# Attention by runs of the sequence and list-scheduled engine orders in a fused attention and hyena kernel

## The chip, the cores and the metric

The kernel runs on one core of one Trainium2 chip. The metric is the device time of one execution in microseconds (us). The kernel before took 243.26 us (median of three executions, 241.11 to 243.58) when the prediction was made.

The engines are called as the profile calls them. PE is the tensor engine with its matmuls, and PEld its weight loads. DVE is the vector engine, ACT the scalar engine, POOL the engine that issues the casting loads, and SP the engine that issues the other loads and the stores. PSUM is the memory that PE writes. It has eight banks, each of 512 float32 values per partition. ACT and DVE read it and so make room for PE.

## The reference

Attention with a window of 96 positions and 8 global positions feeds a projection into three parts. The second part is convolved with a filter along the sequence, which the kernel does as a product of spectra, with the Fourier transforms as matmuls. The other two parts are its gates.

```python
# q, k, v: 4 batches, 8 heads, 768 positions, 64 columns
scores = q @ k.T / 8 - slope[head] * dist        # only kept positions: local or global
a = exp(scores - max); a = a / sum(a)
x = (a @ v), heads side by side                  # 4 x 768 x 512
x1, x2, x3 = split(x @ w_proj)                   # 512 columns each
x2_conv = irfft(rfft(x2) * rfft(filter_fft))     # along the 768 positions
out = (x1 * x2_conv * x3) @ w_out
```

## The kernel before

Everything is issued in an order woven by hand. One batch is attention, head pair by head pair, and then a "hyena" stage: the projection of x2, its spectrum, the product with the filter, the inverse, the gates, and the last projection. The attention of batch b + 1 is woven into the hyena stage of batch b. The gates `x1 * x3` are handed out wherever the stage would let PE wait.

```python
def mm(self):                                   # single-bank products: three banks of their own
    pt = self.ps.tile([P, 512], F32, tag="mm", bufs=3)
    return pt
# scores:     self.ps.tile([P, 2, 512], F32, tag="s",  bufs=1)   one tile of two banks, read as a whole
# values:     self.ps.tile([P, 7, D + 1], F32, tag="av", bufs=2)
# transposes: self.ps.tile([P, 1024], F16, tag="tr", bufs=1)

def gate(j, s):                                 # half s of the sequence, 128 columns j
    p1 = self.mm()
    p3 = self.mm()
    for pt, o in ((p1, 0), (p3, 2 * DM)):
        for c in range(4):
            nc.tensor.matmul(pt[:, 0:h], self.w[:, c, o + P * j:o + P * j + P],
                             xT[:, c, h * s:h * s + h], start=(c == 0), stop=(c == 3))
    x1 = mp.tile([P, h], F16, tag="x1", name="x1")
    nc.scalar.mul(x1, p1[:, 0:h], X1_SCALE)
    nc.vector.tensor_mul(g[:, j, h * s:h * s + h], p3[:, 0:h], x1)

# in the hyena stage ... (cut)
for s in range(6):
    self.forward(s, ab[0], ab[1], evac)         # spectrum of x2
    yield 1
    if s % 2 == 1 and s > 1 and more():         # more(): the next gate, if one is left
        yield 1
for _ in range(2):
    if more():
        yield 1
# ... inverse, with more() between its halves, then the last projection (cut)
```

Attention 0 also issues matmuls on an idle tile (`self.busy(1)`), 38 in all, to keep PE busy. The Fourier tables are computed after attention 0.

The softmax here doesn't subtract the row's maximum and nothing guards it: scores larger than these inputs give would overflow.

## Time and profile before

One execution is read here, with a span of 240.6 us.

| what | value |
|---|---|
| busy | PE 83%, DVE 67%, ACT 60%, POOL 31% |
| attention 0 alone | 0 to 45 us |
| tables, filter, hyena stage 0, attention 1 | 45 to 119 us |
| two mixed periods | 43.7 us each, PE busy 41.5 us in each |
| last hyena stage, alone | 34 us |

The page of the kernel before, its totals and some of its rows of 40 slices (each digit is the busy share of 6 us in tenths; PEclk is the granted clock of PE in tenths):

```profile
span 240.6 us, 4274 instructions
PE 200.6 (83%) x1664; PEld 108.8 (45%) x1664; DVE 161.1 (67%) x334; ACT 144.4 (60%) x232; POOL 75.2 (31%) x102
...
PE   4575968887978665867999999899999997999883
...
PEclk9998597997999995697999999999999999999999
DMA  6999999999991000002999910033000002400006
```

The same execution by stretches. The columns are the stretch, its length, the busy time of PE, PEld, DVE, ACT and POOL with instruction counts, the granted clock, the DMA share and GB/s:

```profile
0.00:45.00 45.00, 31.16 (x278) 16.84 (x278) 30.27 (x70) 21.58 (x28) 35.63 (x55) 0.89 2.00 191
45.00:119.00 74.00, 57.44 (x452) 30.70 (x452) 49.98 (x95) 44.09 (x71) 27.90 (x35) 0.88 1.11 66
119.00:162.70 43.70, 41.62 (x395) 23.43 (x394) 33.09 (x71) 29.98 (x51) 11.66 (x14) 1.00 1.26 99
162.70:206.40 43.70, 41.45 (x391) 23.09 (x388) 33.08 (x71) 29.84 (x50) 0.00 (x0) 1.00 0.10 35
206.40:240.60 34.20, 28.88 (x154) 14.71 (x152) 14.69 (x27) 18.94 (x35) 0.00 (x0) 1.00 0.18 67
```

The two periods in the middle are bound by PE, which is busy for 95% of them. The first 119 us are not. There PE waits, as the chain of waits (start, length, work) of the stretch from 53 us shows, where tables, filter and products follow each other through three engines:

```profile
53.07 1.28 ACT L267
54.36 2.40 ACT fwd L267 x4
57.77 0.70 DVE h_767 L358
58.49 0.59 ACT h_767 L360
```

### The profile page before, as it was taken

Reading aid. Unit: us, or ns where it says so; the run is one execution under the profiler, and the core shown is the slowest. Engines: PE = TensorE matmul, PEld = TensorE weight load, DVE = VectorE, ACT = ScalarE, POOL = GpSimd, SP = SyncE. Lnnn points to the kernel's source line nnn. Section 1 sums busy time; section 2 is a strip of 40 time slices with the busy share of each in tenths; the row PEclk is TensorE's granted clock in tenths of the full one; section 3 lists DMA queues with packets and bytes.
Section 4 is the critical chain, followed back from the end, with each engine's and each line's share of the span. In section 5 each row is a group of like instructions: output and inputs, shape, how many; then the busy total and the mean of one; then the engine's idle time right before and its main releaser. Section 6 shows DMA issues by size and latency. Waiting matters only on the chain.

```text
span 240.6 us, 4274 instructions
## 1 busy us (share of the span) xinstructions
PE 200.6 (83%) x1664; PEld 108.8 (45%) x1664; DVE 161.1 (67%) x334; ACT 144.4 (60%) x232; POOL 75.2 (31%) x102
## 2 busy tenths in 40 slices
PE   4575968887978665867999999899999997999883
PEld 1333545332445342544545565455556554455541
DVE  5587586683675896597246999943599994139550
ACT  4462574477553863573668748466866765774643
POOL 6969478987930000004977200000000000000000
PEclk9998597997999995697999999999999999999999
DMA  6999999999991000002999910033000002400006
GB/s 190 347 132 197 204 155 149 122 171 148 129 119 11 0 3 0 3 0 18 191 246 142 114 10 3 0 143 123 0 3 0 4 0 102 162 0 0 3 34 229
DMA packets 79572, 21.68 MB, mean 90 GB/s; under 512 B 71328, under 2 KB 76480, under 8 KB 79552
## 3 DMA queue, kind: packets, MB, share of 16 engines
q0 software_dynamic: 73584, 11.67, 86.1%
q1 hardware_dynamic: 5968, 9.74, 12.2%
q8 instruction: 13, 0.21, 0.4%
q14 instruction: 7, 0.06, 0.1%
HBM read 26.48 MB, written 6.29 MB: 136 GB/s over the span
## 4 chain that ended last, share of the span: by engine, by line
PE 47%; DVE 23%; ACT 10%; issue 3%; ACTq 0%; DVEq 0%
PE pt L552 9%; PE pt L566 9%; PE pt L649 8%; PE pt L631 5%; PE pt L323 4%; DVE g L557 3%; DVE xn L527 3%; PE sp L490 3%; ACT E_99 L497 3%; PE tx L534 2%; PE o L517 2%; PE o L522 1%; PE tk L478 1%; PE tq L453 1%; DVE X L592 1%
## 5 line engine op out<-in xcount | busy, mean ns | idle before, releaser
L552 PE MATMUL pt<-xT,w 128*128 128x384 f16 x256 | 47.8, 331 | 2.1 <-ACT x_861 L556 1.7
L552 PEld LDWEIGHTS <-w 128*128 128x128 f16 x256 | 24.1, 99 | 18.8 <-issue 4.4
L497 ACT ACTIVATE E_99<-sp 128x864 f16<-128x864 f32 x24 | 21.5, 897 | 13.4 <-PE sp L490 12.7
L649 PE MATMUL pt<-wo,y 128*128 128x512 f16 x96 | 24.4, 396 | 2.6 <-DVE y L642 2.6
L497 ACT ACTIVATE E_96<-sp 128x864 f16<-128x864 f32 x24 | 21.5, 894 | 7.7 <-PE sp L490 7.6
L105 POOL DMA_DIRECT2D vt<-in_v_dram x28 | 25.1, 911 | 2.6 <-DMA kt<-in_k_dram 1.2
L490 PE MATMUL sp<-QT,KT 64*128 64x216 f16 (+2 forms) x224 | 18.5, 258 | 6.4 <-ACT E_99 L497 2.6
L631 PE MATMUL pt<-inv,X 128*128 128x384 f16 x96 | 20.6, 351 | 3.7 <-DVE X L592 3.6
L652 ACT ACTIVATE t<-pt 128x512 f32<-128x512 f32 x24 | 14.3, 597 | 13.7 <-PE pt L649 13.6
L105 POOL DMA_DIRECT2D kt<-in_k_dram x21 | 18.9, 916 | 6.8 <-DMA qt<-in_q_dram 3.3
L527 DVE TENSOR_TENSOR xn<-o,rc 128x448 f16<-128x448 f32 x32 | 20.0, 625 | 1.1
L568 ACT CAST dst<-pt 128x512 f16<-128x512 f32 x24 | 14.1, 587 | 8.8 <-PE pt L566 8.8
L323 PE MATMUL pt<-dst,fwd 128*128 128x512 f16 x72 | 18.9, 380 | 0.0
L275 PE MATMUL pt<-idle 128*128 128x512 f16 x38 | 17.7, 503 | 1.2 <-DVE idle L674 1.2
L535 ACT COPY xT<-tx 128x768 f16<-128x768 f16 x16 | 12.8, 798 | 8.5 <-PE tx L534 8.4
L490 PEld LDWEIGHTS <-KT 64*128 64x128 f16 x224 | 7.8, 96 | 21.9 <-issue 18.6
L595 ACT CAST X<-pt 128x512 f16<-128x512 f32 x24 | 14.1, 587 | 4.9 <-PE pt L323 4.6
L534 PE MATMUL tx<-ident,xn 128*128 128x128 f16 x112 | 9.8, 232 | 8.1 <-DVE xn L527 8.1
L118 POOL DMA_DIRECT2D qt<-in_q_dram x18 | 15.9, 904 | 0.2 <-issue 0.2
L96 POOL MEMSET vt<- 128x56 f16 x4 | 1.6, 412 | 43.3 <-PE o L522 43.3
L649 PEld LDWEIGHTS <-y 128*128 128x128 f16 x96 | 9.1, 102 | 13.2 <-DVE y L642 4.0
L631 PEld LDWEIGHTS <-X 128*128 128x128 f16 x96 | 8.9, 103 | 11.1 <-DVE X L592 4.7
(231 smaller groups left out, 393.5 us busy)
## 6 DMA issues: line engine op xcount, KB each, us to landing
out_dram<-t SPq DMA_DIRECT2D x24, 256.0 KB, 2.6
vt<-in_v_dram POOLq DMA_DIRECT2D x24, 128.0 KB, 7.0
qt<-in_q_dram POOLq DMA_DIRECT2D x18, 128.0 KB, 8.2
kt<-in_k_dram POOLq DMA_DIRECT2D x18, 128.0 KB, 6.5
t<-in_q_dram SPq DMA_DIRECT2D x4, 384.0 KB, 6.1
t<-in_k_dram SPq DMA_DIRECT2D x4, 384.0 KB, 7.1
w<-in_moe_w_proj_dram POOLq DMA_DIRECT2D x3, 512.0 KB, 9.7
fl<-in_moe_filter_fft_dram POOLq DMA_DIRECT2D x1, 768.0 KB, 10.4
```

What stands on the lines that cost most here:

```text
L105: g.dma_start(dst[P - (hi - lo):P, t, :, 0:D], src[b, :, lo:hi, :].rearrange("h p d -> p h d"))
L118: g.dma_start(qt[:, t], self.q[b, :, P * t:P * t + P, :].rearrange("h p d -> p h d"))
L275: self.nc.tensor.matmul(pt, self.idle[:, 0:P], self.idle, start=True, stop=True)
L323: self.nc.tensor.matmul(pt, self.fwd[:, kt, s, :], src[:, kt, :], start=(kt == 0), stop=(kt == 2))
L490: nc.tensor.matmul(sp[:, hh, off:off + w], KT[64 * hh:64 * hh + 64, o:o + P], QT[64 * hh:64 * hh + 64, KL * m:KL * m + w], start=(off == 0 ...
L497: nc.scalar.activation(eo, sp[:, :, 0:432].rearrange("p h (m w) -> p h m w", m=2), Act.Exp, scale=self.scale)
L527: nc.vector.tensor_mul(xn[:, :, hh, :], o[:, :, 0:D], rc.to_broadcast([P, 7, D]))
L534: nc.tensor.transpose(tx[:, KL * t:KL * t + P], xn[:, t, :, :], self.ident)
L552: nc.tensor.matmul(pt[:, 0:h], self.w[:, c, o + P * j:o + P * j + P], xT[:, c, h * s:h * s + h], start=(c == 0), stop=(c == 3))
L566: nc.tensor.matmul(pt, src[:, c, P * t:P * t + P], self.w[:, c, DM:2 * DM], start=(c == 0), stop=(c == 3))
L631: nc.tensor.matmul(pt[:, 0:h], X[:, s, cs], self.inv[:, s, :], start=(s == slots[0]), stop=(s == slots[-1]))
L649: nc.tensor.matmul(pt, y[:, c, P * t:P * t + P], self.wo[:, c, :], start=(c == 0), stop=(c == 3))
```

## The change

Its intent is to let nothing wait for an order fixed by hand. Each operation is handed to a list scheduler with a cost, what it reads and what it writes. The scheduler chooses the order of every engine, which of ACT and DVE empties a bank, and the bank. Attention goes by three runs of the sequence over all head pairs. A run's gates are made as soon as its x is transposed, and no longer inside the hyena stage (now `conv`). Angles and sines of the tables come first, under the first loads. The idle matmuls are gone. The diff of some 1,500 lines, cut to its core:

```diff
+class Plan:                                     # list scheduler (cut)
+    def schedule(self):
+        banks = [0.0] * 8                       # when each of 8 banks is free
+        ...
+                if o.acq:
+                    if o.acq.n == 1:            # a single bank: any of the eight
+                        i = min(range(8), key=lambda i: (max(banks[i], at), banks[i ^ 1] == math.inf
+                                                          and -1 or 0, -banks[i]))
+                    else:                       # scores take two
+                        i = min((0, 2, 4, 6), key=lambda i: max(banks[i], banks[i + 1]))
+        ...
+        self.psum = [self.ps.tile([P, 1024], F32, name=f"bank{i}") for i in range(4)]
+    def emit(self, order):
+        for o in order:
+            a = o.acq
+            if a:
+                lo = 512 * (a.at % 2)
+                a.tile = self.psum[a.at // 2][:, lo:lo + 512 * a.n]
+            o.fn(o.eng)
+
+    def attention(self, b):
+        for c in range(3):                      # runs of the sequence
+            ...                                 # transposes of Q and K, scores, values, transposes of x
+            if c:
+                for j in range(4):
+                    self.gate(b, j, c - 1)      # gates as soon as the run is there
-    def mm(self):
-        pt = self.ps.tile([P, 512], F32, tag="mm", bufs=3)
-        return pt
-        gates = iter([(j, s) for j in range(4) for s in range(2)])
-        def more(): ...                         # gates handed out inside the hyena stage
-                    if first:
-                        self.busy(1)            # idle matmuls
```

## The prediction

> **What bounds the kernel now.** The table of stretches splits the 240.6 us span. 0 to 45 us: attention of batch 0 alone (PE busy 31.2 us, much of it fillers on an idle tile; granted clock 0.89). 45 to 119 us: filter tables, gating stage 0 and attention 1 (PE busy 57.4 of 74 us, clock 0.88). 119 to 206.4 us: two periods of 43.7 us (PE busy 41.5 each, clock 1.00: bound by the tensor engine). Then the last gating stage alone (PE busy 28.9 of 34.2). DVE (67%) and ACT (60%) bound no long stretch. In the first 66 us the page's DMA slices read 9 at some 180 GB/s, about 150 where casting loads run alone: the start is bound by loads, then by the serial chain of filter tables and products (chain of waits, 53 to 95 us), with PE waiting for DVE and ACT.
>
> **What the matmuls need.** From spacings in the timeline (0.216 us at 512 columns, 0.162 at 384, about 0.032 for value products, 0.058 for transposes, score pairs side by side): gating stage 28.7 us, attention 10.3, filter 5.8; 163 us in all. A period's floor is 39 against 43.7.
>
> **What the change does.** Matmuls stay (1,630 in the order listing against 1,664, 38 fillers gone). Sines and forward tables move ahead of attention 0, under the first loads. Gates follow each run of x; conv 0, filter and attention 1 interleave freely; any free PSUM bank serves any product. Some 37 of 52 Q and K copies go to ACT: ACT grows from 144 to about 157 us busy, DVE stays near 161 (16 more reciprocals at 0.2 us, more small copies). Batch 0's Q and K lose their contiguous load: Q comes in 256 byte pieces, K is cast by the POOL queue.
>
> **Sum.** Loads until batch 1's values: Q 1.6 MB at about 300 GB/s, 7 MB by POOL at 150: about 55 us. By then the order has 44 us of PE work. 119 us remain: 101 in mixed periods, which I stretch by 9% (before: 12%) to 110, and the last conv, now without gates to fill its waits: 9.1 (projection, forward) + 4.6 (evacuation, products, sums) + 3.9 + 1.6 + 5.2 + 3.6 (evacuation, store) = 28 us. 55 + 110 + 28 + 2 for a throttled clock = **195 us**, range **186 to 209**. Nearly all the gain lies in the first 119 us (now 75 to 80 for the same work); mixed periods give 2 to 4 us each.
>
> The Trainium skill (TensorE: Matmul & The Clock Gate, Part 1) says that about 3.4 us idle halves the clock. The dips in the clock slices fit; without fillers I expect dips before 35 us.
>
> Chances: faster 0.94, same 0.03, slower 0.03.
>
> **What would show it.** PE busy about 180 us, over 90% from 55 us to the last conv, clock 1.00 there; DMA slices at 9 until about 55; periods of 41 to 43 us; PE waits of 4 to 5 us on DVE sums in the last conv; no long PE wait on ACT sines.
>
> **What would make it wrong.** The fixed orders: if loads land late, PE stands behind a transpose of batch 1 while gates could run (PE waiting for DMA). Small Q pieces slower than 300 GB/s. DVE and ACT, some 80% busy in a shorter span, holding banks (PE waiting for evacuations), so that periods stay at 44. Throttling in 20 to 55 us. Each costs 5 to 15 us.

## The result, and the profile after

The kernel after is correct and takes 234.2 us (median of four executions, 232.63 to 234.45). The kernel before, timed on the same chip in the same rounds, took 242.7 us. The ratio is 0.9651, with a 95% interval of 0.9598 to 0.9705. Ratios in this document are the mean time of one kernel's fast runs over that of the other's fast runs of the same rounds, so they are not quite the ratio of the medians quoted. The change is faster by 3.5%. The predicted 195 us, with a range of 186 to 209, is far off. Most of the expected gain is missing.

The page of the kernel after, same rows as before:

```profile
span 232.7 us, 4288 instructions
PE 190.6 (82%) x1630; PEld 111.4 (48%) x1630; DVE 157.6 (68%) x381; ACT 145.1 (62%) x252; POOL 75.0 (32%) x96
...
PE   5473889798996797899989998999979889991871
...
PEclk9997667999999599999999999999999999999799
DMA  7999999999999979992400000150000001500015
```

The stretches of the kernel after. The last three begin with the conv of batch 1, 2 and 3, up to a microsecond or two:

```profile
0.00:55.00 55.00, 40.60 (x370) 26.68 (x371) 40.86 (x109) 33.86 (x53) 45.11 (x63) 0.88 2.02 167
55.00:113.30 58.30, 49.70 (x444) 29.60 (x442) 41.11 (x96) 38.03 (x70) 29.87 (x34) 0.94 1.44 109
113.30:156.20 42.90, 39.85 (x362) 22.89 (x362) 31.74 (x77) 30.29 (x54) 0.00 (x0) 1.00 0.10 38
156.20:200.30 44.10, 40.39 (x371) 23.62 (x371) 33.38 (x79) 29.43 (x52) 0.00 (x0) 1.00 0.09 32
200.30:232.60 32.30, 20.05 (x87) 8.63 (x85) 10.52 (x20) 13.54 (x27) 0.00 (x0) 0.94 0.19 71
```

PE lost its idle matmuls, but its busy share did not rise. The mixed periods take 43 and 44 us, as before, with PE busy for 92 to 93% of them (95% before). The last conv has PE busy for only 20 of 32 us, where the last stage before had 29 of 34. Its gates, some 10 us of matmuls, are already done, and still it is only 2 us shorter.

Where the trace says that engines waited (engine, tile and line, then what for; us in total, times, longest us), five lines of the kernel after:

```profile
ACT x L310 <- PE bank L682: 14.4, 17, 2.7
...
ACT eo L306 <- PE bank L746: 10.5, 11, 5.7
...
DVE p L795 <- ACT X L306: 10.9, 2, 8.8
...
PE bank L746 <- DVE X L806: 3.7, 1, 3.7
...
PE bank L552 <- DMA kn<-in_k_dram: 3.0, 2, 1.9
```

PE names no single long wait: the largest is 3.7 us, once, in the last conv. So the loss is spread over many short waits, and one has to ask for a reason that acts everywhere. The first line gives a hint. ACT copies the first product of a gate, x1, and waits for PE on it 17 times. Looking at single ones, such a copy often starts 0.65 us later than its own product ends, which is the time of four matmuls of 384 columns: the length of the next product.

One more figure serves below. "PE's own work" is the sum over matmuls started of their spacing at full clock (0.216 us for 512 columns, 0.162 for 384, 0.056 for 128, 0.030 for a value product, score pairs counted side by side). It is 161.1 us for the whole kernel after. The prediction said that 44 us of it would be in the order by 55 us. The trace has 26.8 us of it by then. The other 134.3 us then take 177.7 us, so 1.32 us per us of work, where the prediction had (110 + 28 + 2) / 119 = 1.18. With that rate 26.8 us by 55 us would have given about 213 us. So of the miss of 37.7 us in the span, about 18 lie in the first 55 us and about 20 in the rate after them.

### The profile page after: what moved, and what is told of

It is laid out like the page before. It is cut to its first block, busy times and chain, and to the rows that moved or that the text cites. A ratio compares the mean times of both kernels' runs of the same rounds, so it can differ in the third digit from the quotient of the medians.

```text
span 232.7 us, 4288 instructions
## 1 busy us (share of the span) xinstructions
PE 190.6 (82%) x1630; PEld 111.4 (48%) x1630; DVE 157.6 (68%) x381; ACT 145.1 (62%) x252; POOL 75.0 (32%) x96
## 5 line engine op out<-in xcount | busy, mean ns | idle before, releaser
L682 PE MATMUL bank<-xT,w 128*128 128x384 f16 x256 | 44.3, 329 | 2.6 <-ACT xT L306 1.4
L588 ACT ACTIVATE E<-bank 128x864 f16<-128x864 f32 x48 | 40.1, 903 | 1.6 <-PE bank L578 1.4
L682 PEld LDWEIGHTS <-w 128*128 128x128 f16 x256 | 25.1, 99 | 19.9 <-issue 3.6
L600 DVE TENSOR_TENSOR E<-E,mask 128x864 f16<-128x864 f16 x32 | 18.4, 602 | 17.8 <-ACT E L588 17.7
L322 POOL DMA_DIRECT2D kn<-in_k_dram x28 | 25.4, 920 | 5.5 <-DMA g<-in_moe_filter_fft_dram 2.9
L322 POOL DMA_DIRECT2D vn<-in_v_dram x28 | 25.0, 914 | 2.3 <-PE bank L625 1.4
L746 PE MATMUL bank<-inv,X 128*128 128x384 f16 x96 | 20.9, 364 | 5.4 <-DVE X L806 3.7
L769 PE MATMUL bank<-wo,y 128*128 128x512 f16 x96 | 22.5, 379 | 2.4 <-ACT eo L306 1.0
L640 DVE TENSOR_TENSOR xn<-bank,rc 128x256 f16<-128x256 f32 (+1 forms) x48 | 22.5, 469 | 1.6
L310 ACT ACTIVATE ot<-bank 128x512 f32<-128x512 f32 x24 | 13.4, 595 | 14.3 <-PE bank L769 6.8
L620 PE MATMUL bank<-vn,E 128*128 128x65 f16 x224 | 18.8, 201 | 2.3 <-DVE xn L640 0.7
L539 PE MATMUL bank<-ab,fwd 128*128 128x512 f16 x72 | 18.3, 379 | 1.3 <-ACT ab L306 0.7
L625 PE MATMUL bank<-vn,E 128*128 128x65 f16 x192 | 18.5, 200 | 0.0
```

The costliest lines, as they stand in the source:

```text
L310: self.nc.scalar.mul(out, in_, c)
L322: return self.g.op(eng, {"G": 0.93, "S": 0.5}[eng], lambda _: e.dma_start(dst, src), w=w, r=r, nbytes=nbytes, name=name, bias=-2000.0 + se ...
L588: g.op("A", act(864), lambda _: nc.scalar.activation(eo, b.f32().rearrange("p (h c) -> p h c", h=2)[:, :, 0:432].rearrange("p h (m w) -> p ...
L600: nc.vector.tensor_mul(eo, eo, mk[:, :, 0:2] if gi == 0 else mk[:, :, 1:3])
L620: nc.tensor.matmul(o[:, hh, i], ef[:, at:at + P], vt[:, t, 2 * hp + hh, :], start=first, stop=(t == 0), skip_group_check=True)
L625: nc.tensor.matmul(o[:, hh, i], ef[:, at:at + P], vt[:, t - 1, 2 * hp + hh, :], start=False, stop=True, skip_group_check=True)
```

## Experiments

Fourteen kernels ran, in five groups; kernels of a group shared the runs of the kernel before. In the first and the last group two and three of seven executions of the kernel before were slow, and the record calls the class of all their runs unclear; so the ratios and their intervals are given for every run. Line numbers differ a little between them: the gates are L682 in the kernel after, L684 and L683 in the first two experiments. Where a recorded expectation names a theory by a letter, its own words explain it. The theories in short:

- **Ties.** The banks of the kernel after are halves of two-bank tiles. If what a reader waits for is worked out by tile, a reader of one half also waits for the product in the other half, and "any free bank serves any product" is false.
- **Busy engines.** DVE or ACT, busier in a shorter span, hold the banks.
- **Gates.** Made early, they are no longer there to fill conv's waits.
- **The opening.** Loads, clock, masks or tables hold the first 55 us.

### 1 and 2: banks of their own, and the same order with tied banks

In the first kernel, four single banks are tiles of their own and two tiles of two banks remain, so that the scheduler has six units of which none is half of another. A single product in a two-bank tile takes it whole. The second kernel has the same schedule and the same addresses, but its single banks are again halves of two-bank tiles. Only the naming of the tiles differs between the two.

```diff
+S1 = 4
-   i = min(range(8), key=lambda i: (max(banks[i], at), banks[i ^ 1] == math.inf and -1 or 0, -banks[i]))
+   i = min((*range(S1), *range(S1, 8, 2)), key=lambda i: (max(banks[i], at), i >= S1, -banks[i]))
-   self.psum = [self.ps.tile([P, 1024], F32, name=f"bank{i}") for i in range(4)]
+   # first kernel:
+   self.psum = [self.ps.tile([P, 512], F32, name=f"bank{i}") for i in range(S1)] + [
+       self.ps.tile([P, 1024], F32, name=f"bank{i}") for i in range(S1, 8, 2)]
+   # second kernel: four tiles of [P, 1024] as in the kernel after, the same schedule
```

> The changed kernel with PSUM cut into four tiles of one bank and two tiles of two banks, and the list schedule told so (six units in place of eight banks). Theory A (the two halves of a two-bank tile are tied: a reader of one half waits for matmuls into the other, so the orders slip by some 30 us against their plan): no reader waits late any more, the time falls to 212 to 220 us, x1 copies start about 0.65 us earlier after their product. Theory B (DVE and ACT are too full in the attention parts, ties don't matter): within 1% of 234 us, because six units are fewer than eight banks.

> Control of the run before: the same six units, the same orders on every engine and the same bank addresses, but the four single banks are again halves of two two-bank tiles. Theory A: clearly slower than with own tiles, 224 to 236 us. Theory B: the same as with own tiles within 1%.

Both are correct. The first takes 215.34 us (ratio 0.8941, 0.8856 to 0.9026). The second takes 241.52 us (ratio 1.0037, 0.9942 to 1.0132). Tiles of their own save 0.110 of 241.5 us, which is 26 us, with the same instructions in the same order at the same addresses. The two groups of executions are far apart even with the slow one counted: 215.1 to 219.0 us against 240.6 to 243.1. (The second is also slower than the kernel after. Its schedule was made for six free units which it does not have, while the schedule of the kernel after prefers a bank whose partner is taken. That reason was not tested.)

The timelines show a tie at work. Here are 32 gate matmuls in one row, four pairs of products, and the four x1 copies that read the first product of each pair (start, length). First, tiles of their own:

```profile
116.89 5.36 PE L684 MATMUL bank<-xT,w 128*128 128x384 f16 x32
...
118.09 0.59 ACT L312 ACTIVATE x<-bank 128x384 f16<-128x384 f32 x1
...
119.10 0.49 ACT L312 ACTIVATE x<-bank 128x384 f16<-128x384 f32 x1
120.40 0.49 ACT L312 ACTIVATE x<-bank 128x384 f16<-128x384 f32 x1 [0.81 <-PE bank L684]
121.70 0.49 ACT L312 ACTIVATE x<-bank 128x384 f16<-128x384 f32 x1 [0.81 <-PE bank L684]
```

Then the same four with tied halves:

```profile
129.85 5.36 PE L683 MATMUL bank<-xT,w 128*128 128x384 f16 x32
...
131.18 0.50 ACT L311 ACTIVATE x<-bank 128x384 f16<-128x384 f32 x1
132.06 0.49 ACT L311 ACTIVATE x<-bank 128x384 f16<-128x384 f32 x1
134.01 0.49 ACT L311 ACTIVATE x<-bank 128x384 f16<-128x384 f32 x1 [1.46 <-PE bank L683]
135.31 0.49 ACT L311 ACTIVATE x<-bank 128x384 f16<-128x384 f32 x1 [0.81 <-PE bank L683]
```

Measured from the start of the row of matmuls, the last two copies start at 3.51 and 4.81 us with tiles of their own, and at 4.16 and 5.46 us with tied halves. Both are 0.65 us later, which is four matmuls of 0.163 us: the second product of the pair, into the other half. The built program says the same without a clock. Of 187 reads of PSUM that wait on PE in the kernel after, 79 wait for a later matmul than the last one that wrote their own bank, by 510 matmuls in sum. In the second kernel it is 53 of 217, in the first 0 of 254. Only reads were counted. Writes into one half may be tied to reads of the other as well. Each late copy also gives its bank back late.

### 3: the products with the masks taken away

All mask products, 48 operations in 64 DVE instructions, are left out of the kernel after. DVE's busy time falls from 157.6 to 131.7 us.

> The changed kernel without the mask products (48 multiplications, some 28 us of VectorE work; the result is wrong on purpose), orders kept. Theory B: 8 us or more off. Theory A: below 6 us, since the work taken away has little to do with the late waits.

It takes 233.69 us (ratio 0.9706, two executions, so one look). Nothing moved: DVE does not bound the kernel after. ACT was not relieved here. But in experiments 1 and 2 both engines have the same work, and the times are 26 us apart.

### 4: half of the gates' matmuls taken away

Each gate product of the kernel after sums two of its four parts (`for c in range(2)`), which takes away 20.8 us of PE's own work.

> The changed kernel with two of the four contraction steps of each gate product left out (20.8 us of matmuls at full clock; the result is wrong on purpose), orders kept. If the tensor engine's own work bounds most of the span: 15 us or more off. If it mostly waits (theories A and B): 5 to 14 us off; gates stand where x1 waits for the second product of the pair, so theory A gives some of it back too.

It takes 222.36 us (ratio 0.9235), one look. Of 20.8 us of matmuls 10 to 12 came off the time, so PE does not pace all of the span. This fits short waits spread all over. It doesn't say what share PE paces, since the gates taken away are also where x1 waits.

### 5 and 6: the gates back into the conv

In the kernel of experiment 1, and in the kernel after, the gates move from the attention to conv's list, where the scheduler may still place them as it likes:

```diff
 def attention(self, b): ...
-            if c:
-                for j in range(4):
-                    self.gate(b, j, c - 1)
 def conv(self, b): ...
+        for j in range(4):
+            self.gate(b, j, 0)
         self.spectra(b, (2, 3))
         self.spectra(b, (4, 5))
+        for j in range(4):
+            self.gate(b, j, 1)
```

> Own tiles as in u_own (215.3 us), but the gates are put back into the conv of their batch (the second named part of the change undone). Theory C (gates are the only matmuls that wait for nothing late in the conv; done early they leave the conv's serial chain bare, above all at the end of the last batch): 202 to 209 us, and the last conv has no gap of 4 us before the inverse products. Theory D (early gates help, as announced, since they fill attention's waits): 217 us or more.

> The changed kernel with its eight banks in four tied tiles, with gates back in the conv. Theory C: 221 to 229 us against 234. Theory D: 236 us or more. If ties and gates are separate causes, the ratio to the changed kernel is about that of v_gconv to u_own.

With tiles of their own it takes 204.52 us (202.86 to 205.94; ratio 0.8459, 0.8379 to 0.8538), correct. With tied tiles, the second takes 218.87 us (ratio 0.9064, 0.8984 to 0.9144), correct; its profiled execution was slow. Between ratios, the gates are worth 0.8941 - 0.8459 = 0.048 (12 us) with free banks, and 0.9651 - 0.9064 = 0.059 (14 us) with tied ones. The two faults together cost 0.119 (29 us), a little less than the sum of each alone.

The page and the stretches of the faster one:

```profile
PE 185.2 (92%) x1630; PEld 108.8 (54%) x1630; DVE 153.0 (76%) x383; ACT 147.2 (73%) x250; POOL 75.2 (37%) x96
...
PE   5676897999995999999999999999999999999972
```

```profile
0.00:55.00 55.00, 46.06 (x402) 28.66 (x403) 43.56 (x119) 38.61 (x58) 45.34 (x63) 1.00 2.12 165
55.00:80.00 25.00, 22.70 (x181) 12.51 (x179) 22.20 (x50) 22.93 (x42) 16.89 (x20) 1.00 2.01 119
80.00:165.00 85.00, 84.17 (x885) 51.56 (x884) 70.10 (x182) 64.00 (x112) 13.00 (x15) 1.00 0.59 67
165.00:202.40 37.40, 32.29 (x168) 16.06 (x165) 17.11 (x34) 21.67 (x40) 0.00 (x0) 1.00 0.22 85
```

From 80 to 165 us PE is busy 84.17 of 85 us. This is what the prediction had expected from 55 us on. The last stretch has 32 of 37 us, not 20 of 32: with gates to fill them, the waits of the last conv (for the DVE sums) are no longer on show. But that is not all of the gain. From the first matmul of the last conv to the end it takes 36.1 us, against 30.3 in experiment 1, with 12.4 us more of PE's own work in it (44 matmuls of gates, and 24 of the last projection of the batch before): 6.6 us gained there. The other 4.4 of the 11 us between the two spans were gained before it. There the whole order is new, so what gained them is not shown.

### 7: idle matmuls for the clock

The clock row of the kernel after dips several times before 45 us, as the prediction expected without the idle matmuls. So the kernel of experiment 1 got idle matmuls, in gaps of the order's first 36 us. The trace shows 26 more matmuls than without; where the expectation gives a larger number, it was counted wrongly.

> u_own with 52 filler matmuls on an idle tile, placed in the first 36 us where the schedule leaves the tensor engine idle. If the half clock at 20 to 27 us costs what its length says: 2 to 5 us less than u_own (210 to 213 us) and a granted clock of 1.00 to 70 us. If the start is bound by loads and by the ScalarE chain: within 1.5 us of u_own.

It takes 218.48 us (ratio 0.9066, 0.8994 to 0.9139; 0.8941 without them), correct. That is about 3 us slower by the ratios, whose intervals just overlap, and no gain. The clock was full from 13.5 us to 71.5 us. But the idle matmuls themselves are 13.5% of the chain of work that ended last in the first 40 us, so they also held back the work that they were meant to speed up.

### 8 and 9: masks later, tables later

In experiment 8 the masks are no longer all built ahead of the first exponentials, but two behind each of them, in the kernel of experiment 1. Experiment 9 has this, the gates in conv, and the tables moved back behind attention 0, at the price of one more table load of ACT.

```diff
-        for h in range(self.H):  ...            # all eight masks, before the exponentials
+        self.masks(2, [e])                      # two behind each of the first ones
-        self.tables(); self.load_first(); self.attention(0)
+        self.load_first(); self.attention(0); self.tables()       # experiment 9 only
```

> u_own with the eight mask exponentials no longer in one block of 5.2 us ahead of the first score exponentials, but two of them behind each of the first ones. If that block holds up attention 0: 2 to 4 us less than u_own. If attention 0 waits for its loads anyway: within 1 us.

> v_gconv (204.5 us) with the filter tables taken out of the start again: score exponentials first, angles, folds and sines after batch 0's last exponential (one more table load of 1.28 us), and masks behind the first exponentials. If the early tables help, as my prediction had it: 207 us or more. If they only trade places with attention 0, whose casts wait for the folds: within 2 us of v_gconv. If they hold attention 0 up: 202 us or less.

Experiment 8 takes 215.27 us (ratio 0.8898, 0.8809 to 0.8987), the same as experiment 1. Experiment 9 takes 203.86 us (ratio 0.8432, 0.8367 to 0.8498), the same as experiment 5 (0.8459). In experiment 9 attention 0 begins earlier (first scores at 11.7 us, not 16.9) and ends earlier (last value product at 33.0 us, not 37.3). But the tables then follow it. Early tables, which the change names as a gain, only trade places with attention 0.

### 10 and 11: the loads of batch 0 taken away

First, the K and V loads of batch 0 were replaced by fills on POOL in the kernel of experiment 5. Then, in the kernel of experiment 9, one tile of K and two of V stood for the other eleven, with no fill.

> v_gconv with the 14 loads of batch 0's K and V replaced by fills of the same tiles on the same engine at the same place (the result is wrong on purpose); weights and batch 1 come 5 to 10 us earlier. If loads bound the first 55 us, as my prediction had it: 8 us or more less than v_gconv. If attention 0's own chain from engine to engine bounds it: 4 us or less.

> v_gcmt with the loads of batch 0's K and V cut to one K tile and two V tiles, which stand for all the others (wrong on purpose; 11 of 14 loads gone, and no fill put in their place). It mends the earlier run without these loads, where fills on POOL took their place and a DVE instruction of 0.55 us stood for 4.58 us beside them. Theory C (ACT and DVE bound the opening): 203 to 206 us, last value product of batch 0 still at 31 to 34 us. Theory D (loads bound it): the value product moves ahead by 4 us or more and the time falls by 3 us or more, to 201 us or less.

The first takes 206.99 us (ratio 0.8547), but it is spoiled. Its fills on POOL ran from 9.85 to 14.09 us, and a DVE instruction beside them stood still. The same instruction in this kernel, and in the kernel of experiment 5, from which it was made:

```profile
9.93 4.58 DVE L418 TENSOR_SCALAR eo<-eo 128x768 f32<-128x768 f32 x1
```

```profile
8.86 0.55 DVE L411 TENSOR_SCALAR eo<-eo 128x768 f32<-128x768 f32 x1
```

The Trainium skill (SBUF — State Buffer, Who interferes with whom) says that DVE in a two-port mode and the engine that the profile calls POOL share a port pair, and that one of them fully blocks. This agrees: 4.58 us for 0.55, and it ended at 14.51 us, 0.42 us after the last fill. (The mode of the DVE instruction is not in the trace.) This was the reason to repeat the experiment without fills. The second kernel takes 205.85 us (ratio 0.8550, 0.8485 to 0.8616), against 0.8432 for experiment 9. It gained nothing and was somewhat slower. But the scheduler made another order for it, in which the value products of batch 0 begin at 37.6 us and not at 21.7, and PE is at half clock until 33.7 us and not until 22.7. So neither run is clean: together they show that fewer loads of K and V brought no gain, not that these loads never hold anything. Q's loads were not tried.

### 12: no masks at all

In the kernel of experiment 9, from 12 to 33 us, ACT and DVE are nearly full: ACT is busy 18.75 of 21 us and DVE 18.77. So masks were left out altogether, their building on ACT (6 us) and their products on DVE.

> v_gcmt (203.86 us) without masks: neither the eight mask exponentials on ACT (about 6 us, in the first 20 us) nor the 32 mask products on DVE (about 19 us in all, 7 us of them in batch 0). Wrong on purpose. In v_gcmt, from 12 to 33 us, ACT is busy 18.75 of 21 us and DVE 18.77, PE 15.3. Theory C (the opening is bound by ACT and DVE work of attention 0, not by loads): the last value product of batch 0 moves from 33.0 us to 27 to 30 us, PE's ideal work by 40 us rises from 18.9 us to 21 or more, and the time falls by 3 to 6 us, to 198 to 201 us. Theory D (loads bound the opening): nothing moves, 203 to 205 us. Theory E (the opening's gain is eaten later, since the tables and the filter follow anyway): the value product moves but the time falls by less than 2 us.

It takes 201.25 us (ratio 0.8323, 0.8208 to 0.8437, against 0.8432), about 2.6 us less, within the intervals. The stretch from 12 to 33 us, first in the kernel of experiment 9, then without masks:

```profile
12.00:33.00 21.00, 15.31 (x210) 10.52 (x209) 18.77 (x53) 18.75 (x26) 16.50 (x20) 1.00 1.80 180
```

```profile
12.00:33.00 21.00, 15.34 (x182) 10.16 (x180) 13.49 (x36) 11.83 (x14) 16.93 (x21) 1.00 1.78 184
```

DVE and ACT were relieved by 5 and 7 us, and PE did no more in the stretch (15.3 us). Half of the value products of batch 0 had come by 26.0 us instead of 27.8, but the last came at 33.9 us instead of 33.0. The expected 198 to 201 us were just missed, and so was the earlier last value product. (The expectation counts only the larger 32 of the 64 mask products.) The work of DVE and ACT, taken as a sum, does not hold the opening alone.

### 13 and 14: the clock of the opening once more

The clock row of experiment 5's page reads full clock from the start, but its trace has no clock record before 36.8 us. The matmuls tell another story. Six score matmuls in the kernel of experiment 5 at 30 us, and six in the same kernel with idle matmuls (start, length of the row):

```profile
30.25 0.54 PE L580 MATMUL bank<-QT,KT 64*128 64x216 f16 x6
```

```profile
29.49 0.36 PE L581 MATMUL bank<-QT,KT 64*128 64x216 f16 x6
```

Equal matmuls follow each other at 1.9 times the full-clock spacing until 36 us in experiment 5, and until 23 us in experiment 9. So both kernels got idle matmuls in gaps of the order, 43 in the first 36 us of experiment 5, and 20 in the first 24 us of experiment 9.

> v_gconv (204.5 us) with 43 filler matmuls of 512 columns in gaps of the order's first 36 us. By the spacing of equal matmuls the tensor engine of v_gconv runs at half clock until about 36 us of the trace, though the page's clock line, which has no record before 36.8 us, shows full clock there; its matmuls do about 0.7 us of full-clock work in every 2 us until then. Theory T (half clock holds the opening): with fillers the spacing is full from about 12 us on, PE's own work by 40 us rises from 15.9 to 19 us or more, and the time falls by 3 us or more, to 201.5 us or less. Rival C (ACT and DVE of attention 0 hold it, as they read 18.8 of 21 us busy in v_gcmt, whose clock was full from 23 us on): the clock rises and the time stays, 203 to 207 us.

> v_gcmt (203.9 us; half clock until about 23 us by the spacing) with 20 filler matmuls in gaps of the order's first 24 us. Theory T: full clock from about 12 us on, the last value product of batch 0 moves from 33.0 to 30 us or earlier, and the time falls by 2 us or more, to 202 us or less. Rival C: no gain, 203 to 206 us.

They take 206.0 us (ratio 0.8539, 0.8436 to 0.8641; 0.8459 without) and 202.57 us (ratio 0.8369, 0.8270 to 0.8469; 0.8432 without; its profiled execution was slow), both correct. Neither differs from its base beyond the intervals. In the second, the profiled execution fell back to half clock at 14.3 and 34.8 us, so only the first is a test of the clock. There, spacings are full from about 10 us on, yet the last value product of batch 0 comes at 37.3 us, to the tenth where it was at half clock. PE's own work by 40 us was not more either: by one and the same sum it is some 15.5 us in both. But this does not clear the half clock. In the first 40 us of the first kernel's trace the idle matmuls (L879) are 26.7% of the chain of work that ended last, the largest part of it: they stood in front of the work, as in experiment 7. Idle matmuls did not help; what the half clock costs the opening stays open.

## Why the prediction was wrong

The direction was right, but 234.2 us lies far outside 186 to 209. Point by point:

- **"Any free PSUM bank serves any product": this step failed, and it is the largest.** The prediction read the scheduler's list of eight banks and did not read that they are halves of four tiles. In the built program, readers of one half wait for the product in the other. Experiments 1 and 2 price it at 26 us for one and the same order. Against the kernel after, six free units instead of eight tied ones save 0.071, about 17 us. The prediction had named waits for evacuations as a danger, and gave engines that are too busy as its cause. Experiment 3 shows that DVE is not it, and experiments 1 and 2 have 26 us between them with the work of both engines the same. The symptom came true, with another reason.
- **"Mixed periods" at 1.09 of their matmuls, 41 to 43 us: the mechanism was right, and the tie hid it.** The kernel after has 42.9 and 45.0 us from conv to conv. With free banks (experiment 1) it is 40.2 and 41.0.
- **Gates follow each run: counted as harmless but for the last conv; this step failed too.** They are matmuls that wait for nothing late in the conv. Leaving them in conv's list is worth 12 to 14 us (experiments 5 and 6), of which the last conv of experiment 5 shows 6.6; the rest was gained earlier, in an order that is new as a whole. The last conv alone was put at 28 us. It measured 33 us in the kernel after and 30 us with free banks.
- **"By then the order has 44 us of PE work": mis-sized.** It assumed that PE goes through its order as loads land. The kernel after did 26.8 us by 55 us, and experiments 5 and 9 did 30 to 33 us. This is the remainder once both faults are mended. In experiment 5, 30.1 us were done by 55 us, and the other 131.0 us took 147.4, so 1.125 per us, which is better than the 1.18 of the prediction. The missing 14 us in the opening are thus more than all of the distance from 195 to the span of 202.4. They were lost before 40 us: between 40 and 55 us experiment 5 did some 14 us of work in 15. Masks and the early tables were each tried and neither holds the opening alone. Idle matmuls for the clock and fewer loads of K and V brought nothing, in runs that are not clean. What holds it stays open. The trace of experiment 9 speaks for the loads: its chain of work that ended last by 40 us is, until 23.6 us, mostly POOL issuing the loads of K and V and then the landing of a load, and after that mostly the engine-to-engine work of attention 0. In experiment 12 a load of Q is 20.8% of that chain. PE ran at half clock in both, until 22.7 and 25.3 us. Loads, the work from engine to engine and the half clock were not separated from each other.
- **Loads done by about 55 us: right as an event, wrong as a sign.** The last V of batch 1 landed at 53.5 us. But the DMA row does not fall there; it reads 9 in nearly every slice until about 110 us, because the loads of the next batch follow at once. (The 300 GB/s for Q was an estimate. The page of the kernel before has 9.74 MB in queue q1 with 12.2% of 16 engines' span, which is 332 GB/s.)
- **Busy times: DVE 157.6 (predicted 161), ACT 145.1 (157).** PE's busy time of 190.6 us instead of 180 has the half clock in it. The matmul work itself was 161.1 us, against 163 predicted.
- **Clock.** Dips before 35 us came. The Trainium skill (TensorE: Matmul & The Clock Gate, Part 1) gives a window of about 3.4 us and half the clock after an idle one. The dips of the kernel after last 6.8 us, twice before 38 us and once at 75, and 3.4 us, once in the last conv, so the length agrees. The condition does not. Of these four only the dip in the last conv, at 215.0 us, follows 3.4 us without a matmul. Before the other three (20.4, 30.7 and 75.0 us) PE was busy, by the profile, for 2.1, 2.5 and 1.8 of the 3.4 us, and in the kernel before for 1.2 to 1.4 ahead of each of its five dips. The measurement decides: here PE lost its clock without an idle window. "Clock 1.00 from 55 us" failed (0.94 in two stretches) for want of work. Its price is not known: three kernels with idle matmuls gained nothing beyond the intervals (experiments 7, 13 and 14), but the idle matmuls stood in the chain themselves.
- **PE waits of 4 to 5 us on DVE sums in the last conv:** seen, a little shorter, once 3.7 us. **No long wait on sines:** right.

The best kernels that ran are experiments 5, 9 and 14, at about 202.5 to 204.5 us, correct and about 16% faster than the kernel before. They do not differ from each other beyond their intervals. Of the change they keep the runs, the scheduler and the loads. They undo the early gates and the halved tiles.

## What to carry to other kernels

When an allocator hands out parts of a buffer, check in the built program what a reader of one part waits for. A copy that starts later by just the length of the neighbour's product is a sign of a tie, and giving each unit a buffer of its own may be worth more than having more units. Matmuls that wait for nothing can fill the waits of a latency-bound stage, so try leaving them in that stage's list before running them as early as possible. And when predicting, count what PE can do in the opening from what the chain releases, not from what the order holds.

## What the Trainium skill lacked or had wrong

- PSUM — Partial Sum Buffer, PSUM bank collisions raise a hardware error: it tells to guard PSUM by bank and gives no price for guarding it more coarsely. Here waits by two-bank tile, with the same order and addresses, cost 26 us of 241.5 (experiments 1 and 2), and 79 of 187 reads waited for matmuls of another bank.
- TensorE: Matmul & The Clock Gate, Part 1: it asks for an idle window of about 3.4 us before the clock is halved. In the kernel after three dips follow 3.4 us with PE busy for 1.8 to 2.5 of them. It doesn't say either that idle matmuls can stand in the way of the work: in experiment 13 they were 26.7% of the chain in the first 40 us and brought no gain, though the clock was full from about 10 us on.
- The same page warns against trusting single clock records, and calls half clock the default. It lacks that before the first clock record the profile's clock row can read full while PE runs at half clock. Here that was until 36.8 us, with 0.54 us for six score matmuls against 0.36 at full clock. Take the spacing of equal matmuls instead.
- ScalarE: Activation LUTs, What ACT_TABLE_LOAD costs: about 2.66 us with a drain of 1.38. In experiment 9 the table load took 1.28 us, and the first sine began 1.29 us after it did (28.93 to 30.22), straight behind exponentials. No drain is to be seen there.
